# Attention, an expert network and a cosine network in one kernel: the merged unit goes last, and conversions, weights' jobs and pair products stand in other places

## The chip, the cores and the metric

The kernel runs on one core of a Trainium2 chip. The time is the device time of one execution in microseconds (us). A kernel's time is the median of several executions; one further execution is recorded by the profiler, and every row below comes from that one.

## What is computed

Three stages follow each other; the output of each is the input of the next (all float32 for the reader; `w_in` and `w_out` come as float64).

```python
scores = scale * np.matmul(q, k.transpose(0, 1, 3, 2))      # B=2, H=8, S=576, D=64
scores = np.where(mask, scores + bias[None], -1000000000.0) # causal window of 128, ALiBi slopes
attn = softmax(scores); x = attn @ v                        # -> 1152 tokens x 512
for e in range(4):                                          # w1[e] 512x1024, w2[e] 1024x512
    h = np.maximum(x @ w1[e], 0.0)
    out += p[:, e:e + 1] * (h @ w2[e])                      # p: normalised domain_probs
h = out @ w_in                                              # 512 x 2048
result = (h * np.cos(h)) @ w_out                            # 2048 x 512
```

## The kernel before

**Precision.** Every operand of the two networks is held as two parts, a high part that TensorE takes and a low part, the remainder. A product is three passes (high-high, high-low, low-high), so that 128 contraction rows of a 128x512 result cost three matmuls. The high part is a ScalarE copy, the low part a subtract (`sub`, L162), on DVE for some and on GpSimd for others.

**Tokens.** The 1152 tokens are nine units of 128 (`UNITS`, `place`): unit 0 holds the first 64 rows of both batches, merged; units 1 to 4 are the rest of batch 0, units 5 to 8 the rest of batch 1. The networks use the same nine as tiles; tiles 1 to 4 and 5 to 8 are the two halves of a 2x2 block product.

**Attention.** Each unit has two steps (`steps`, four heads each). In a software pipeline, step k computes its scores (`att_scores`, L418), the transposes of the probabilities come two steps later, the product with the values another one later, and the unit's normalised result (L530) is then transposed and cut into the operands of the networks (`own`, `transform`). Between these pieces `fill(k, s)` puts other work by a table of steps: the jobs that cut the weights (k 4 to 19), the transposed constants, and the first products of group 0.

**The two networks.** The first one runs in groups 0 to 7 (four experts, halves of F1), the second in groups 8 to 11 (quarters of 2048); each group has 512 hidden columns. A group has these parts:
- Two `pair`s (j = 0, 1), layer one for tiles 1 to 8 in Winograd's form: seven products A11, A12, S1, S2, S3, S4, A22 of six matmuls 128x512 each (L647, `product`). A11 and A12 add into the same PSUM bank; between them ScalarE copies the bank into p1 (L717). DVE forms u1, c22 and the final sums (L711). `finish` makes the hidden values: a ReLU in the first network; in the second a cosine chain of six stages (`cosine`, L595: two ScalarE steps, DVE's L604, ScalarE's sine L608, DVE's product with h, then ScalarE's high part L620 and GpSimd's low part L162).
- `left`: layer one of tile 0, two blocks of twelve matmuls 128x256 (L677), and `turn_rows` ("X" in the tables): its four transposes (L703) and the cut into parts.
- `layer2` per tile, twelve matmuls (L787), then one DVE sum into `acc` (L808, L814). In the second network `ahead` ("a5" to "a8") does half of tiles 5 to 8 early.

The operands named in the rows: `xs` and `xz` are the cut token operands, `w1t` and `w2t` the cut weights, `hpair` and `h0` the hidden values of tiles 1 to 8 and of tile 0, `x0` the operands of tile 0.

**What sets the order.** `tc.manual_schedule()` keeps the order of the code on each engine. `steps(g)` yields a list of (step, stages, njobs, ncv), and `run` (L974) issues for each: the first half of the step (its matmuls), `stages` stages of every open cosine chain, `njobs` weights' jobs, `ncv` steps of conversions, then the second half (its copies and sums). A weights' job is a ScalarE part and a GpSimd subtract, with a raw load on the SyncE queue. A conversion (`convert`, L254) turns the 64-bit words of `w_in` and `w_out` into float32 in DRAM: a load on the SyncE queue into one of two buffers, ScalarE L272 and L284, DVE L274, L278, L282 and L287 in four steps, and a store; 32 of them have to be done by the end of group 6, since the second network's weights are read from there.

**The turn.** In group 7 the accumulated tiles are the input of the second network: `flip` ("f0" to "f7", then `last_flip`) transposes a finished tile and cuts it like the attention's units, between the layer-two steps of that group.

## Time and profile before

| | |
|---|---|
| three runs | 686.02, 686.30, 689.27 us; median 686.3 |
| the profiled execution | 689.04 us; its span 687.3 us |
| TensorE (PE) busy | 651.2 us, 95% of the span; weight loads (PEld) 77% |
| VectorE (DVE) busy | 453.6 us, 66% |
| ScalarE (ACT) busy | 329.6 us, 48% |
| GpSimd (POOL) busy | 350.8 us, 51% |
| mean granted TensorE clock | 0.987 of 2.4 GHz |

A row of a timeline reads: start, duration, engine, line, operation, output<-input, shape, how many instructions stand in the row; in brackets the idle time of the engine before it, the engine that ended that wait, and what it wrote. The modelled end of a matmul row can lie some 0.15 us behind the start of the next row, since matmuls are pipelined; so the time between two starts is what a row costs.

### The profile page before, as it was taken

Reading aid. Unit: us, or ns where it says so; the run is one execution under the profiler, and the core shown is the slowest. Engines: PE = TensorE matmul, PEld = TensorE weight load, DVE = VectorE, ACT = ScalarE, POOL = GpSimd, SP = SyncE. Lnnn points to the kernel's source line nnn. Section 1 sums busy time; section 2 is a strip of 40 time slices with the busy share of each in tenths; the row PEclk is TensorE's granted clock in tenths of the full one; section 3 lists DMA queues with packets and bytes.
Section 4 is the critical chain, followed back from the end, with each engine's and each line's share of the span. In section 5 each row is a group of like instructions: output and inputs, shape, how many; then the busy total and the mean of one; then the engine's idle time right before and its main releaser. Section 6 shows DMA issues by size and latency. Waiting matters only on the chain.

```text
span 687.3 us, 9161 instructions
## 1 busy us (share of the span) xinstructions
PE 651.2 (95%) x3332; PEld 528.9 (77%) x3332; DVE 453.6 (66%) x778; ACT 329.6 (48%) x687; POOL 350.8 (51%) x330
## 2 busy tenths in 40 slices
PE   8999979999899999999999999998999989989988
PEld 6776758888688888788788888886777677767766
DVE  5778968968868878868773624557844743753652
ACT  5877534553353453444442422556663654653640
POOL 2755617365255274174364561753487377368340
PEclk9999999999999999999999999999999999999999
DMA  7441204625615516446231210110102102001003
GB/s 240 115 138 48 65 28 137 215 62 181 187 31 185 183 51 224 124 124 196 78 123 47 61 62 31 37 56 0 31 1 92 31 0 93 31 1 61 17 5 118
DMA packets 38957, 60.38 MB, mean 88 GB/s; under 512 B 4608, under 2 KB 21248, under 8 KB 38912
## 3 DMA queue, kind: packets, MB, share of 16 engines
q1 hardware_dynamic: 38912, 59.80, 27.2%
q8 instruction: 26, 0.43, 0.3%
q14 instruction: 19, 0.16, 0.1%
HBM read 49.04 MB, written 10.75 MB: 87 GB/s over the span
## 4 chain that ended last, share of the span: by engine, by line
PE 42%; DVE 22%; ACT 12%; DMA 8%; issue 7%; POOL 7%; SPq 1%; POOLq 0%; DVEq 0%; ACTq 0%
PE o_ps L787 20%; PE o_ps L647 15%; DMA cr<-w_in 5%; DMA cr<-w_out 4%; POOL w1t L162 2%; PE o_ps L677 2%; DVE o_ps L711 2%; DVE cv L278 2%; DVE c L711 2%; DVE cv L282 2%; DVE hpair L637 2%; ACT p L435 2%; POOL w2t L162 2%; ACT hpair L636 2%; ACT u L608 1%
## 5 line engine op out<-in xcount | busy, mean ns | idle before, releaser
L787 PE MATMUL o_ps<-w2t,hpair 128*128 128x512 f32 x1140 | 270.7, 393 | 6.0 <-POOL hpair L162 5.0
L787 PEld LDWEIGHTS o_ps<-w2t,hpair 128*128 128x128 f32 x1140 | 212.3, 189 | 50.8 <-POOL hpair L162 6.8
L647 PE MATMUL o_ps<-xs,w1t 128*128 128x512 f32 x720 | 173.8, 397 | 10.5 <-ACT p L717 7.3
L647 PEld LDWEIGHTS o_ps<-xs,w1t 128*128 128x128 f32 x720 | 136.4, 191 | 42.5 <-ACT p L717 10.2
L162 POOL TENSOR_TENSOR w1t<-raw,w1t 128x512 fp32r<-128x512 f32 x48 | 63.7, 1342 | 102.1 <-ACT w1t L185 101.8
L162 POOL TENSOR_TENSOR w2t<-raw,w2t 128x512 fp32r<-128x512 f32 x48 | 66.7, 1406 | 81.9 <-ACT w2t L185 81.6
L647 PE MATMUL o_ps<-xz,w1t 128*128 128x512 f32 x288 | 72.5, 401 | 8.1 <-DVE c L711 7.7
L162 POOL TENSOR_TENSOR w1t<-sm,w1t 128x512 fp32r<-128x512 f32 x48 | 64.1, 1345 | 20.6 <-ACT w1t L185 19.0
L647 PEld LDWEIGHTS o_ps<-xz,w1t 128*128 128x128 f32 x288 | 54.3, 192 | 24.4 <-DVE c L711 12.3
L162 POOL TENSOR_TENSOR hpair<-u,hpair 128x512 fp32r<-128x512 f32 x32 | 42.8, 1355 | 54.6 <-ACT hpair L620 54.6
L808 DVE SCALAR_TENSOR_TENSOR accpair<-o_ps,pr,accpair 128x512 f32<-128x512 f32 x56 | 41.6, 744 | 32.9 <-PE o_ps L787 32.9
L637 DVE SCALAR_TENSOR_TENSOR hpair<-o_ps,hpair 128x512 fp32r<-128x512 f32 x48 | 32.9, 688 | 21.6 <-ACT hpair L636 21.5
L185 ACT ACTIVATE w1t<-sm 128x512 fp32r<-128x512 f32 x44 | 27.4, 626 | 39.5 <-POOL sm L162 39.5
L272 ACT ACTIVATE cr<-cr 128x512 int32<-128x512 uint32 x32 | 21.7, 679 | 48.9 <-DMA cr<-w_out 24.8
L636 ACT ACTIVATE hpair<-o_ps 128x512 fp32r<-128x512 f32 x48 | 28.5, 597 | 33.6 <-DVE o_ps L711 33.0
L604 DVE SCALAR_TENSOR_TENSOR u<-r,u 128x512 f32<-128x512 f32 x36 | 33.8, 938 | 15.2 <-ACT r L601 15.1
L677 PE MATMUL o_ps<-w1t,x 128*128 128x256 f32 x288 | 39.9, 285 | 1.9 <-POOL w1t L162 1.9
L435 ACT ACTIVATE p<-p,nmax 128x256 f32<-128x256 f32 (+2 forms) x72 | 33.5, 468 | 16.5 <-DVE nmax L429 16.5
L677 PEld LDWEIGHTS o_ps<-w1t,x 128*128 128x128 f32 x288 | 37.7, 191 | 4.5 <-POOL w1t L162 2.9
L284 ACT ACTIVATE cr<-cr 128x512 f32<-128x512 f32 x32 | 21.7, 678 | 37.8 <-DVE cv L278 37.7
L814 DVE TENSOR_TENSOR accpair<-o_ps,accpair 128x512 f32<-128x512 f32 x23 | 15.9, 690 | 36.1 <-PE o_ps L787 36.1
L711 DVE TENSOR_TENSOR o_ps<-o_ps,u 128x512 f32<-128x512 f32 x48 | 33.2, 691 | 6.7 <-PE o_ps L647 6.7
(134 smaller groups left out, 895.7 us busy)
## 6 DMA issues: line engine op xcount, KB each, us to landing
raw<-w SPq DMA_DIRECT2D x32, 512.0 KB, 3.7
cr<-w_in SPq DMA_DIRECT2D x16, 512.0 KB, 4.4
cr<-w_out SPq DMA_DIRECT2D x16, 512.0 KB, 4.4
wi<-cv SPq DMA_DIRECT2D x16, 256.0 KB, 3.4
wo<-cv SPq DMA_DIRECT2D x16, 256.0 KB, 2.2
raw<-wi SPq DMA_DIRECT2D x8, 512.0 KB, 3.4
raw<-wo SPq DMA_DIRECT2D x8, 512.0 KB, 3.6
qt<-qT SPq DMA_DIRECT2D x9, 256.0 KB, 2.9
```

The source lines that it names most:

```text
L162: eng.tensor_tensor(out=out, in0=a, in1=b, op=ALU.subtract)
L185: nc.scalar.activation(out=out, in_=src, func=AF.Copy)
L272: nc.scalar.activation(out=lw, in_=lw.bitcast(U32), func=AF.Copy, scale=2.0 ** -29)
L435: nc.scalar.activation(out=p[:, k, :wid], in_=p[:, k, :wid], func=AF.Exp, scale=-1.0, bias=nmax[:, k : k + 1], accum_out=den[:, k, 0:1],)
L604: nc.vector.scalar_tensor_tensor(out=u, in0=r, scalar=MAGIC, in1=u, op0=ALU.subtract, op1=ALU.subtract)
L636: nc.scalar.activation(out=hi, in_=src, func=AF.Relu)
L637: nc.vector.scalar_tensor_tensor(out=lo, in0=src, scalar=0.0, in1=hi.bitcast(F32), op0=ALU.max, op1=ALU.subtract)
L647: nc.tensor.matmul(ps, w(a, k, m), operand_of_x(bb, b)[:, m], start=(start and m == 0 and (a, bb) == PASSES[0]), stop=(stop and m == 1 and ...
L677: nc.tensor.matmul(ps[:, j * 256 : (j + 1) * 256], x0[:, bb, d, :], w_t[1, g, j][:, a, 0, d * 256 : (d + 1) * 256], start=(d == 0 and (a, ...
L711: add = lambda out, a, b: nc.vector.tensor_tensor(out=out, in0=a, in1=b, op=ALU.add)
L787: nc.tensor.matmul(ps, hidden(a, f, t), w_t[2, g, f // 2][:, bb, f % 2, :], start=(f == 0 and (a, bb) == PASSES[0]), stop=(f == NFG - 1 an ...
L808: nc.vector.scalar_tensor_tensor(out=o, in0=ps, scalar=s, in1=o, op0=ALU.mult, op1=ALU.add)
```

## The change

1. The attention's units run in the order 1 to 8, then 0. Unit 1 is loaded in halves, its keys on the ScalarE queue; unit 0's keys have a tile of their own (`kh`). The small bias `bm0` is built at k = 9, the identity before that.
2. Group 0's left rows, their transposes, the routing and tile 0's layer two leave the attention and stand in `steps(0)`; the pairs of group 0 start at k = 18 and 19.
3. `pair` has three kinds: 0 puts A12 after S3 (groups 1 to 7, as before), 1 puts it right after A11 (groups 0 and 8), 2 after S2 and u1 (groups 9 to 11, which had it right after A11).
4. In groups 9 and 10 two weights' jobs stand in the second pair in place of beside "a5" and "a6".
5. At the turn, the left rows of group 8 leave the tiles and stand in `last_flip`, between the first products of both pairs; their transposes ("X") and tile 0's layer two stand inside group 8's pairs.
6. Conversions stand only beside the tiles and left rows that the table `ncv` names, none beside tiles 3 and 4 and "X": 23 steps in a group.

```diff
+        make_identity(nc, ident)
+
+    def first_bias():
+
         for b in range(2):
             r = slice(64 * b, 64 * b + 64)
             nc.gpsimd.tensor_copy(bm0[r], bm[r, :, WIN + 64 * b : WIN + 64 * b + 64])
-        make_identity(nc, ident)
...
     def load_unit(u):
...
         if u == 0:
+            nc.sync.dma_start(out=qt, in_=blocks(qT, 0, 128))
+            kh = qvp.tile([128, B, ND, 64], F32, name="kh", tag="qt")
...
+                nc.sync.dma_start(out=kh[:, b], in_=head(b))
+            heads.append(kh)
+            return
...
+        for h in (slice(0, 2), slice(2, 4)) if u == 1 else (slice(0, ND),):
+            nc.sync.dma_start(out=qt[:, h], in_=blocks(qT, u, 128)[:, h])
+            queue = nc.scalar if u == 1 else nc.sync
+            queue.dma_start(out=kt[:, h, s0 : s0 + n], in_=blocks(kT, u, 128)[:, h])
+            if i == 1:
+                queue.dma_start(out=kt[:, h, :64], in_=head(b)[:, h])
...
     def own(t, x1):
 
         hi, lo = parts(t)
+        if t < NP and mm is None:
+            yield
+            yield
         hi(B11, x1[:, 0:2])
         yield
...
-    units = range(1 + 2 * NP)
+    units = [*range(1, 1 + 2 * NP), 0]
...
-    def pair(g, j, early=False):
+    def pair(g, j, early=0):
 
         w = operand(w_t[1, g, j])
         c = lambda name: cp.tile([128, NB], F32, name=name, tag="c")
@@ -716,7 +734,7 @@
         p1 = p1p.tile([128, NB], F32, name="p1", tag="p1")
         nc.scalar.activation(out=p1, in_=pa, func=AF.Copy)
         yield
-        if early:
+        if early == 1:
             product(pa, w, A12, B21, False, True)
             yield
             finish(g, pa, f, 1)
@@ -727,6 +745,11 @@
         u1 = c("u1")
         add(u1, pb, p1)
         yield
+        if early == 2:
+            product(pa, w, A12, B21, False, True)
+            yield
+            finish(g, pa, f, 1)
+            yield
         pc = sums()
         product(pc, w, S1, T1, True, True)
         yield
@@ -872,7 +895,6 @@
             )
         load_units_to(2)
         constants()
-        first = left(0)
         early = {}
 
         def fill(k, s):
@@ -884,23 +906,17 @@
             if (k, s) == (2, 0):
                 for _ in range(RAWS):
                     loads_ahead()
-            if (k, s) == (4, 0):
+            if (k, s) == (6, 0):
                 nc.sync.dma_start(out=pr, in_=probs.rearrange("(t p) e -> p t e", p=128))
-            if (k, s) == (11, 0):
-                routing()
+            if (k, s) == (9, 0):
+                first_bias()
             if s == 0 and 4 <= k < 20:
                 next(jobs)
-            if (k, s) in ((8, 1), (10, 1)):
-                next(first)
             step = None
-            if (k, s) == (10, 2):
-                whole(first)
-            if (k, s) == (13, 1):
-                step = turn_rows(0)
-            if s == 1 and k in (18, 19):
-                step = early[k - 18] = pair(0, k - 18, True)
-            if (k, s) == (20, 2):
-                step = layer2(0, 0, ps_s.tile([128, DM], F32, name="s_ps", tag="s_ps"))
+            if (k, s) == (18, 1):
+                step = early[0] = pair(0, 0, 1)
+            if (k, s) == (19, 1):
+                next(early[0])
             if step:
                 next(step)
             move(24 if (k, s) == (20, 2) else (0, 3, 2)[s])
@@ -923,53 +939,73 @@
 
         last, turn = g == NG1 + NG2 - 1, g == NG1 - 1
         moe = g < NG1
+        early_kind = 1 if g in (0, NG1) else 0 if moe else 2
+        ps = [early.pop(j, None) or pair(g, j, early_kind) for j in range(2)]
         if g == 0:
-            seq = [0, 1] + [0] * 5 + [1] * 5
-            more = [0] * 7 + [1] * 5
+            next(ps[0])
+            yield ps[1], 1, 0, 0
+            yield ps[1], 1, 0, 0
+            first = left(0)
+            yield half(first, False), 1, 0, 0
+            yield half(first, True), 1, 0, 0
+            seq = [0, 0, "X", 0, 0, 0, 1, 1, 1, 1, 1]
+            more = [0] * 6 + [1] * 5
+            routing()
         elif g == NG1:
-            seq = [1, 0, 1] + [0] * 5 + [1] * 5
-            more = [0] * 4 + [1, 1, 0, 0] + [0] * 5
+            seq = [0, 0, 0, 0, "X", 0, 1, 1, "0", 1, 1, 1]
+            more = [0, 1, 1, 0, 0, 0, 1, 1, 0, 0, 0, 0]
+        elif moe:
+            seq = [0] * 7 + [1] * 7
+            more = [0, 1, 1, 0, 0, 0, 0] + [0, 1, 1, 1, 1, 1, 1]
         else:
-            seq = [0] * 7 + [1] * 7
-            more = [0, 1, 1, 0, 0, 0, 0] + [0] + [moe] * 6
-        ps = [early.pop(j, None) or pair(g, j, g == 0 or not moe) for j in range(2)]
-        for k, (j, m) in enumerate(zip(seq, more)):
-            if not moe and k == len(seq) - seq[::-1].index(0):
-                yield layer2(g, 0), 2, 0, 0
-            yield ps[j], 1, int(m), 0
+            seq = [0] * 7 + ["0"] + [1] * 7
+            more = [0, 1, 1, 0, 0, 0, 0, 0] + ([0] * 7 if last else [0, 1, 1, 0, 0, 0, 0])
+        for j, m in zip(seq, more):
+            if j == "X":
+                yield turn_rows(g), 2, m, 0
+            elif j == "0":
+                yield layer2(g, 0), 2, m, 0
+            else:
+                yield ps[j], 1, m, 0
         nxt = None if last else left(g + 1)
+        ncv = {0: 2, "La": 3, 5: 3, 6: 3, 1: 3, 7: 3, "Lb": 2, 2: 2, 8: 2}
         if turn:
-            order = (0, 1, "f0", 5, "f1", 2, "f5", "La", 6, "f2", "Lb", 3, "f6", 4, "f3", 7, "X", "f4", 8, "f7")
+            order = (0, 1, "f0", 5, "f1", 2, "f5", 6, "f2", 3, "f6", 4, "f3", 7, "f4", 8, "f7")
             njobs = [2, 2, 0, 2, 0, 2]
         elif moe:
-            order = (() if g == 0 else (0,)) + ("La", 5, 6, 1, 7, "Lb", 2, 8, 3, "X", 4)
+            order = (0, "La", 5, 6, 1, 7, "Lb", 2, 8, 3, "X", 4)
             njobs = [2] + [1] * 7 if g == 0 else [1] * 8
         elif last:
             order, njobs = ("a5", "a6", "a7", "a8", 5, 6, 7, 8, 1, 2, 3, 4), []
         else:
             order = ("a5", "a6", "a7", "a8", "La", 5, 6, 7, "Lb", 8, 1, 2, "X", 3, 4)
-            njobs = [1, 1, 0, 0, 1, 1, 1, 1, 1, 1, 1, 1, 1, 1, 2]
+            njobs = [0, 0, 0, 0, 1, 1, 1, 1, 1, 1, 1, 1, 1, 1, 2]
         for k, o in enumerate(order):
             m = njobs.pop(0) if njobs else 0
             if isinstance(o, int):
                 assert o == 0 or not any(c > 0 for c, _ in chains)
-                yield layer2(g, o), 2, m, 3 if o == 5 else 2
+                yield layer2(g, o), 2, m, ncv.get(o, 0)
             elif o[0] == "f":
                 yield flip(int(o[1])), 0, m, 0
             elif o[0] == "a":
                 yield ahead(g, int(o[1])), 2 if last else 1, m, 0
             elif o[0] == "L":
-                yield half(nxt, o == "Lb"), 2, m, 2
+                yield half(nxt, o == "Lb"), 2, m, ncv.get(o, 0)
             else:
-                yield turn_rows(g + 1), 2, m, 1
+                yield turn_rows(g + 1), 2, m, 0
         if turn:
-            yield from last_flip(g + 1)
-
-    def last_flip(g):
-
-        early[0] = pair(g, 0, True)
+            yield from last_flip(g + 1, nxt)
+
+    def last_flip(g, nxt):
+
+        early.update({j: pair(g, j, 1) for j in range(2)})
         yield early[0], 0, 0, 0
         yield flip(2 * NP), 0, 0, 0
+        yield early[1], 0, 0, 0
+        yield half(nxt, False), 0, 0, 0
+        yield early[0], 1, 0, 0
+        yield half(nxt, True), 0, 0, 0
+        yield early[1], 2, 0, 0
 
     def run(groups):
         for g in groups:
```

**How the order moves.** Numbers behind a name tell buffers apart.

TensorE, first pair of group 10, before (`o_ps` are PSUM banks, w1t the group's first cut weights):

```order
L647 MATMUL o_ps_5162<-xs_132,w1t_4966 128x512 x12
L647 MATMUL o_ps_5184<-xs_132,w1t_4966 128x512 x6
L647 MATMUL o_ps_5197<-xs_132,w1t_4966 128x512 x6
L647 MATMUL o_ps_5207<-xs_132,w1t_4966 128x512 x6
L647 MATMUL o_ps_5197<-xz_1003,w1t_4966 128x512 x6
L647 MATMUL o_ps_5207<-xz_1003,w1t_4966 128x512 x6
L787 MATMUL o_ps_5244<-w2t_5154,h0_140 128x512 x6
```

TensorE, the same place, after:

```order
L665 MATMUL o_ps_5168<-xs_132,w1t_4897 128x512 x6
L665 MATMUL o_ps_5177<-xs_132,w1t_4897 128x512 x6
L665 MATMUL o_ps_5168<-xs_132,w1t_4897 128x512 x6
L665 MATMUL o_ps_5203<-xs_132,w1t_4897 128x512 x6
L665 MATMUL o_ps_5212<-xs_132,w1t_4897 128x512 x6
L665 MATMUL o_ps_5203<-xz_872,w1t_4897 128x512 x6
L665 MATMUL o_ps_5212<-xz_872,w1t_4897 128x512 x6
```

Before, A11 and A12 stand in one row of twelve on one bank, then S2, S1, S3, S4, A22. After, S2 (o_ps_5177) stands between A11 and A12 (both o_ps_5168), and the other four keep their order.

DVE, from the last tiles of group 2 to the first pair of group 3, before (`cr` and `cv` are conversion buffers, L808 the sums of tiles, L162 the low part of tile 0's hidden values, L711 the pair's sums):

```order
L282 ISA cv_2374<-cr_2331,cv_2374 128x1024
L808 SCALAR_TENSOR_TENSOR accpair_1284<-o_ps_2379,pr_138,accpair_1284 128x512
L287 SCALAR_TENSOR_TENSOR cv_2374<-cr_2331,cv_2374 128x512
L162 TENSOR_TENSOR h0_140<-l_ps_2395,h0_140 128x512
L274 TENSOR_SCALAR cv_2419<-cr_2372 128x512
L278 SCALAR_TENSOR_TENSOR cv_2419<-cr_2372,cv_2419 128x512
L282 ISA cv_2419<-cr_2372,cv_2419 128x1024
L808 SCALAR_TENSOR_TENSOR accpair_1284<-o_ps_2403,pr_138,accpair_1284 128x512
L711 TENSOR_TENSOR u1_2444<-o_ps_2434,p1_2432 128x512
L711 TENSOR_TENSOR c22_2457<-o_ps_2446,u1_2444 128x512
```

DVE, the same place, after:

```order
L302 SCALAR_TENSOR_TENSOR cv_2349<-cr_2320,cv_2349 128x512
L289 TENSOR_SCALAR cv_2390<-cr_2347 128x512
L293 SCALAR_TENSOR_TENSOR cv_2390<-cr_2347,cv_2390 128x512
L831 SCALAR_TENSOR_TENSOR accpair_1235<-o_ps_2373,pr_138,accpair_1235 128x512
L831 SCALAR_TENSOR_TENSOR accpair_1235<-o_ps_2395,pr_138,accpair_1235 128x512
L177 TENSOR_TENSOR h0_140<-l_ps_2409,h0_140 128x512
L831 SCALAR_TENSOR_TENSOR accpair_1235<-o_ps_2416,pr_138,accpair_1235 128x512
L729 TENSOR_TENSOR u1_2449<-o_ps_2439,p1_2437 128x512
L729 TENSOR_TENSOR c22_2462<-o_ps_2451,u1_2449 128x512
L729 TENSOR_TENSOR c22_2462<-o_ps_2464,c22_2462 128x512
```

Before, four conversion instructions stand after the sum on o_ps_2379 and ahead of u1; after, the last one stands ahead of four sums, and between it and u1 stand only those and the parts of tile 0's hidden values.

TensorE, the end of the attention, before (L520 is the values' product of unit 8, s_ps_1231 tile 0's layer two, the rows of L647 are A11 and A12 of both pairs, S2, S1 and S3):

```order
L520 MATMUL x_ps_1205<-pt_1177,vt_893 64x128 x2
L520 MATMUL x_ps_1205<-pt_1177,vt_1005 64x128 x2
L787 MATMUL s_ps_1231<-w2t_1028,h0_140 128x512 x6
L787 MATMUL s_ps_1231<-w2t_1125,h0_140 128x512 x6
L647 MATMUL o_ps_1142<-xs_132,w1t_353 128x512 x2
L647 MATMUL o_ps_1190<-xs_132,w1t_460 128x512 x6
L647 MATMUL o_ps_1306<-xs_132,w1t_353 128x512 x6
L647 MATMUL o_ps_1315<-xs_132,w1t_353 128x512 x6
L647 MATMUL o_ps_1324<-xs_132,w1t_353 128x512 x6
```

TensorE, the same place, after (L527 is the merged unit's values' product, L695 group 0's left rows, L721 their transposes):

```order
L527 MATMUL x_ps_1183<-pt_1118,v0_190 64x64 x4
L527 MATMUL x_ps_1183<-pt_1123,v0_190 64x64 x4
L527 MATMUL x_ps_1183<-pt_1155,v0_190 64x64 x4
L527 MATMUL x_ps_1183<-pt_1160,v0_190 64x64 x4
L665 MATMUL o_ps_1243<-xs_132,w1t_465 128x512 x12
L695 MATMUL o_ps_1260<-w1t_360,x0_133 128x256 x12
L695 MATMUL o_ps_1260<-w1t_465,x0_133 128x256 x12
L665 MATMUL o_ps_1291<-xs_132,w1t_360 128x512 x6
L665 MATMUL o_ps_1300<-xs_132,w1t_360 128x512 x6
L721 MATMUL l_ps_1309<-ident_126,lt_1285 128x128 x4
L665 MATMUL o_ps_1316<-xs_132,w1t_360 128x512 x6
```

Before, tile 0's layer two stands between the last unit and the rest of the first products. After, the merged unit's values' product is the attention's last, group 0's left rows stand between the first products of the second pair and S2, and their transposes between S1 and S3.

## Rows read from the trace of the kernel before

**Rows 1.** TensorE's timeline in group 10; columns as told above.

```profile
579.28 1.52 PE L647 MATMUL o_ps<-xs,w1t 128*128 128x512 f32 x6
581.49 5.73 PE L647 MATMUL o_ps<-xs,w1t 128*128 128x512 f32 x24 [0.69 <-ACT p L717]
587.53 3.04 PE L647 MATMUL o_ps<-xz,w1t 128*128 128x512 f32 x12 [0.31 <-DVE c L711]
590.41 2.88 PE L787 MATMUL o_ps<-w2t,h 128*128 128x512 f32 x12
593.13 1.52 PE L647 MATMUL o_ps<-xs,w1t 128*128 128x512 f32 x6
595.63 5.74 PE L647 MATMUL o_ps<-xs,w1t 128*128 128x512 f32 x24 [0.98 <-ACT p L717]
...
604.55 5.60 PE L787 MATMUL o_ps<-w2t,hpair 128*128 128x512 f32 x24
...
610.93 0.98 PE L677 MATMUL o_ps<-w1t,x 128*128 128x256 f32 x6 [0.54 <-POOL w1t L162]
...
614.66 3.92 PE L787 MATMUL o_ps<-w2t,hpair 128*128 128x512 f32 x16 [1.26 <-POOL hpair L162]
...
632.61 1.52 PE L647 MATMUL o_ps<-xs,w1t 128*128 128x512 f32 x6
```

**Rows 2.** All engines' timeline in group 10: rows of DVE and GpSimd.

```profile
599.19 2.98 POOL L162 TENSOR_TENSOR hpair<-u,hpair 128x512 fp32r<-128x512 f32 x2 [1.64 <-ACT hpair L620]
599.37 1.66 DVE L604 SCALAR_TENSOR_TENSOR u<-r,u 128x512 f32<-128x512 f32 x1
...
600.95 0.68 DVE L711 TENSOR_TENSOR c<-o_ps,u 128x512 f32<-128x512 f32 x1
...
604.58 0.68 DVE L604 SCALAR_TENSOR_TENSOR u<-r,u 128x512 f32<-128x512 f32 x1
...
609.14 3.00 POOL L162 TENSOR_TENSOR w1t<-raw,w1t 128x512 fp32r<-128x512 f32 x2
...
612.09 3.76 POOL L162 TENSOR_TENSOR hpair<-u,hpair 128x512 fp32r<-128x512 f32 x3
```

**Rows 3.** TensorE's timeline, the start of two neighbouring groups of the first network.

```profile
373.57 6.96 PE L647 MATMUL o_ps<-xs,w1t 128*128 128x512 f32 x30
...
420.50 6.96 PE L647 MATMUL o_ps<-xs,w1t 128*128 128x512 f32 x30
```

**Rows 4.** TensorE's timeline at the turn, start of group 8.

```profile
478.60 7.32 PE L647 MATMUL o_ps<-xs,w1t 128*128 128x512 f32 x24 [2.27 <-ACT p L717]
```

**Rows 5.** TensorE's waits, 130 to 440 us (total, times, longest); one from its timeline.

```profile
PE o_ps L647 <- DVE c L711: 4.9, 3, 2.6
...
188.01 4.60 PE L647 MATMUL o_ps<-xz,w1t 128*128 128x512 f32 x12 [2.57 <-DVE c L711]
```

**Rows 6.** DVE's timeline ahead of that hole; DVE's waits from 150 to 186 us.

```profile
185.82 0.74 DVE L808 SCALAR_TENSOR_TENSOR accpair<-o_ps,pr,accpair 128x512 f32<-128x512 f32 x1
...
DVE cv L274 <- DMA cr<-w_out: 2.4, 1, 2.4
```

**Rows 7.** Windows: length, busy PE PEld DVE ACT POOL, granted clock, DMA share, GB/s.

```profile
184.00:192.00 8.00, 5.43 (x18) 3.99 (x17) 6.31 (x9) 1.71 (x3) 1.35 (x1) 0.79 0.41 116
478.00:486.00 8.00, 7.32 (x24) 5.56 (x24) 5.74 (x8) 5.19 (x12) 2.69 (x3) 0.79 0.00 0
```

**Rows 8.** DVE's timeline in the attention: the normalisations of units 5 and 8.

```profile
58.43 0.68 DVE L530 TENSOR_TENSOR x<-x_ps,rs 128x512 f32<-128x512 f32 x1
...
83.75 0.68 DVE L530 TENSOR_TENSOR x<-x_ps,rs 128x512 f32<-128x512 f32 x1
```

**Rows 9.** TensorE's timeline from the start to group 1's left rows.

```profile
9.62 1.65 PE L418 MATMUL s_ps<-k,qt 64*128 64x192 f32 x8
...
89.54 5.95 PE L647 MATMUL o_ps<-xs,w1t 128*128 128x512 f32 x18 [3.17 <-ACT hpair L636]
...
105.88 1.59 PE L677 MATMUL o_ps<-w1t,x 128*128 128x256 f32 x12
```

More of the change, by code (lines that the diff above doesn't have):

```diff
@@ L120, in place, with blocks, head @@
         return (u - 1) // NP, (u - 1) % NP + 1
+    def blocks(a, u, n):
+        return a[:, u * ND * 128 : u * ND * 128 + ND * n].rearrange("p (m n) -> p m n", m=ND)
+    def head(b):
+        o = b * ND * 64
+        return kT[:, o : o + ND * 64].rearrange("p (m n) -> p m n", m=ND)
+    heads = []
     def load_unit(u):
-        q_t[u] = qvp.tile([128, ND, 128], F32, name="qt", tag="qt")
-        cols = slice(u * ND * 128, (u + 1) * ND * 128)
-        nc.sync.dma_start(out=q_t[u], in_=qT[:, cols].rearrange("p (m n) -> p m n", m=ND))
+        qt = q_t[u] = qvp.tile([128, ND, 128], F32, name="qt", tag="qt")
@@ L413, in att_scores @@
                             ps[hh][c, m, :wid], q_t[u][r, 2 * g + m, c],
-                            k_t[b][r, 2 * g + m, :64], start=True, stop=True,
+                            heads[0][r, b, 2 * g + m], start=True, stop=True,
                         )
@@ L447, in att_sums @@
         nc.vector.tensor_reduce(
-            out=rec, in_=dens[:, u % 2], axis=mybir.AxisListType.X, op=ALU.add
+            out=rec, in_=dens[:, units.index(u) % 2], axis=mybir.AxisListType.X, op=ALU.add
         )
```

32 lines of the change are left out of this document (13 added, 19 removed).

## The prediction

> **What bounds the kernel now.** I read the stretches first, then TensorE's timeline for every place where a row starts later than the row before it ends, then the engine that the waiting row names, on its own timeline.
>
> In a middle group of the first network TensorE has no hole: from one group's first product to the next's is 420.50 − 373.57 = 46.93 us [rows 3], and twelve 128x512 products take 593.13 − 590.41 = 2.72 us, 0.227 each [rows 1]. That is all its work, so 46.93 is the floor of a group. A group of the second network takes 632.61 − 579.28 = 53.33 [rows 1]: 6.4 us of holes, in a group that has the same products. Three kinds make them up.
> - After A11 (six products, 1.36 us) A12 should start at 580.64 and starts at 581.49: 0.85. It adds into the bank that ScalarE is still copying (p1). In the second pair it is 595.63 − 594.49 = 1.14.
> - S4 waits for DVE's c22: 24 products from 581.49 end at 586.93, S4 starts at 587.53: 0.60, in both pairs; each hole costs some 0.15 more at the restart. DVE was late because the cosine's L604 stood ahead of c22 and took 1.66 us beside a GpSimd subtract, against about 0.7 otherwise [rows 2].
> - The next left rows wait for w1t (0.69 and 0.55 around 610.93), and tile 5's second half waits for the hidden low part until 614.66 (1.45). GpSimd did two w1t subtracts at 609.14, ahead of the low parts at 612.09 [rows 1, 2].
>
> In the first network three of the seven later groups have a hole, 4.9 us in all [rows 5], each from DVE reaching c22 late: it reads tile 4's sum only at 185.82, after conversion steps that themselves waited 2.4 us for a load [rows 6], and TensorE goes on at 188.01, after which twelve products take 4.60 instead of about 3.0. The granted clock is 0.79 of 2.4 GHz there (part of the stretch at 1.2), after a hole of 2.6 us [rows 5, 7]. With the clock and the restarts I count 7.4 us lost there. The turn to the second network has the same pattern: a hole of 2.27 at 478.60 and 24 products in 7.32 (floor 5.44) at 0.79 [rows 4, 7].
>
> In the attention TensorE runs without holes in its first half, and DVE sets the pace in the second: its normalisation of unit 5 starts at 58.43, that of unit 8 at 83.75 [rows 8], and S2 of group 0 waits until 89.54 [rows 9].
>
> **The change part by part.**
>
> *Kind 2 pairs (groups 9 to 11).* S2 now stands between A11 and A12, so p1 (0.6 us) is hidden by 1.36 us of products: −0.85 and −1.14. c22 stands ahead of L604 on DVE, and S3 still lies between S1 and S4: c22 takes 0.7 of those 1.36, so the 0.60 goes in the first pair. Four restarts of 0.15 go too: 0.6.
>
> *Two weights' jobs from behind the pairs into the second pair (groups 9, 10).* w1t is then ready before the left rows: −0.69 − 0.55. The price: GpSimd's two subtracts (1.25 to 1.5 each [rows 2]; 1.3 taken) lie beside the second pair, and L604 takes 1.66 there rather than 0.68, one microsecond in front of the second add of c22, on which A22 waits. Of that S4 hides about 0.35, so about 0.65 of the second 0.60 is given back. Tile 5's low part now has two w1t subtracts less ahead of it (2.6 us on GpSimd, about 1.0 of copies on ScalarE), but TensorE comes 4.5 us sooner: in the trace of before the low part is there 614.66 − 604.40 = 10.3 us after A22's end, without those jobs about 8, plus the 1.0 from L604; TensorE needs it 5.44 + 1.43 + 0.45 = 7.3 after A22. I keep a wait of 1.7, a little over the 1.45 of now. Sum for one group: 0.85 + 1.14 + 0.60 + 0.6 + 1.24 + (0.60 − 0.65) − 0.25 = 4.1, with the smaller restart costs 4.3. Bounds: 5.5 (DVE's add is not delayed, low part at 7.8) and 2.5 (the low part comes no sooner against the clock on the wall). Two groups: **−8.6**, from −11 to −5.
>
> *Group 11* has no jobs for later groups: the same without w1t, 0.85 + 1.14 + 1.2 + 0.6, and tile 5's wait changes little: **−4**, from −5.8 to −2.
>
> *Turn and group 8.* The left rows (two blocks of 1.43) and the transposes of their result leave the turn's tiles and stand between A11, A12 and their twins. From the last flip to S2 TensorE then has A11', left, A12, left, A12': 1.36 × 3 + 1.43 × 2 = 6.9 us of work, where it now stands still for 2.27 (and loses 7.32 − 5.44 = 1.9 to the clock and restart) [rows 4, 7]. That hole goes, 4.2. Against it: the cosine of the left rows now stands on DVE and ScalarE in front of c22 (two more L604 of 0.7, two more ScalarE steps each of 0.6), so S4 of the first pair waits about 1.7; and the turn's flips follow each other faster by 3.3 us, over which DVE, busy some 5.5 of each 6.1 us, may lose 1. The wait for tile 5's low part (1.3 there too) and the one behind S4 shrink by 1 each, and so does the 0.3 at the left rows' transposes. I take **−4.5**, from −7 to −2.
>
> *Conversions with early tiles only (groups 0 to 4).* 23 steps instead of 24 a group, none beside tiles 3 and 4 and the transposes between. The steps are the same instructions, and DVE is in order; the sum of its work falls by one step (0.7 to 1.4 us). What moves is the order: after the last step DVE now has the reads of tiles 8, 3 and 4 and then u1 and c22, and no load of a conversion can hold these up. Today three to five conversion instructions, one of them behind a load of 2.4, stand there. I expect c22 to come 1 to 2.5 us sooner against TensorE. Of the three holes two are near 1.2 and go; the third of 2.6 shrinks to about 1 and then costs no clock. **−5**, from 0 (the loads, two buffers deep, set the end of the steps wherever they stand) to −7.4.
>
> *The merged unit last.* Before unit 1's scores at 9.62 lie the merged unit's scores [rows 9]; with its transposes and its values' products it takes TensorE about 6 us, and the left rows of group 0 inside the attention 2 × 1.43 (a row of twelve takes 1.59 with the end of the last [rows 9]) and their transposes 0.4. All this no longer stands ahead of unit 5: its normalisation, 58.43 now, comes at about 48.5 [rows 8]. From there DVE sets the pace: 83.75 − 58.43 = 25.3 to unit 8, plus the merged unit's own steps on DVE (two rounds of eight short passes and copies, about 2), plus 5 for unit 8's transform: the merged unit is normalised at about 81. Then x0's two parts (ScalarE 0.6, GpSimd 1.3), A12' waiting behind them on ScalarE, and left rows of 2.86 stand in front of S2: 87 to 88, against 89.54. A hole of 3 to 4 us before A12' stays, as now, with the clock at its lower level after it. But tile 0's layer two (2.72) and the transposes (0.44), which are done by then now, come after S2. So the left rows of group 1 at 105.88 move to about 104.4: **−1.5**. Bounds: −5 if the second half is less DVE-bound than the 25.3 say, +3 if the start gains only the merged unit's own 6. The keys of unit 1 on ScalarE's queue, the halves of its loads and the identity built before the small bias lie in front of the first score, and I count them in the 10.
>
> The sum: −1.5 − 5 − 4.5 − 8.6 − 4 = −23.6. The profiled execution took 689.0 (span 687.3), so 665.4; two of the three other runs were at 686.0 and 686.3, so this execution may hold 2.7 that the median does not, and part of that may be among the holes counted here. I take 665.
>
> **A rule against this change.** L604 with two inputs in SBUF took 1.66 beside a GpSimd subtract; DVE's adds with one input in PSUM stayed near 0.7 [rows 2]. The Trainium skill, "SBUF — State Buffer", section "Who interferes with whom", says that a VectorE instruction with two SBUF inputs contends with a GpSimd instruction that reads SBUF, and that whichever starts first holds the port for its whole length while the other is blocked. By that rule the moved jobs can also be the ones that wait. The row agrees on the slowdown of DVE; which one is blocked in the second pair no row of before can show.
>
> **The rivals.**
> 1. *The low parts become the bound.* Jobs and low parts queue on GpSimd in the second pair, each of the two w1t subtracts and of the four L604 holds up the other by 1.0 to 1.3, and tile 5 waits for what the pair saved: groups 8 to 11 keep 1 to 2 us each, not 4. For it: GpSimd would be busy without a break there; against: its eight low parts and two jobs are 13 us in 24. Time: 665.4 + 4 × 2.5 = 675. Chance 0.17. (The rule above would act in this way.)
> 2. *The conversions do not come earlier.* Their loads set the pace, the three holes stay: 665.4 + 5 = 670. Chance 0.12. A stronger form of it is the slower side: packed three to a tile, each of the six conversions of a group, not one or two, waits 2.4 for its load [rows 6]. That is 4 × 2.4 = 9.6 us more on DVE per group in five groups; with 18.6 saved elsewhere the kernel is slower than now as soon as DVE loses 3.7 a group, and at 9.6 the time is 665.4 + 5 + 48 = 718. Against it: the tiles without steps give DVE 6 us to catch up. Chance 0.04.
> 3. *More from the attention.* The second half is TensorE's again, S2 starts near 82 at the full clock: 665.4 − 5 − 2 = 658. Chance 0.12.
>
> **How the numbers follow.** My forecast (660 to 669) has 0.49, rivals 1, 2 and 3 together 0.41, the slow form 0.04, something that I did not see 0.06 (0.04 of it near no change, 0.01 on either side). From 657 to 677 holds rival 3 and rival 1 and leaves the slow forms out. Faster by over 0.5% (about what the measurement can tell from no change), that is under 682.9: 0.91; within: 0.04; slower: 0.05.
>
> **What would show it.** In the profile after: a second-network group of about 49 us (53.33 now), no wait of the product after A11 on p1, and a wait of under 2.5 us on the hidden low part; first-network groups 1 to 5 at 46.9 to 48; no hole at the first S2 of group 8, but one of 1 to 2 at its S4; the first left rows of group 1 near 104. I am wrong if c22 is late again in the first network, if the low parts' wait grows beyond 3 us, or if S2 of group 0 starts after 90.

## The result and the profile after

The changed kernel takes 669.56 us (median; 668.5 to 672.75) against 686.75 before: a ratio of 0.975, interval 0.971 to 0.979. 665 was forecast, in a range from 657 to 677. The profiled execution took 668.5 us (span 666.7), 20.5 less than the profiled one of before; that pair lies 3 us wider apart than the medians.

Cut at the same marks (group 1's first product, group 7's, group 9's, group 11's), the two traces and one more of the unaltered changed kernel (experiment 6) say where the time went:

| stretch | before | after | after, again | forecast change | seen |
|---|---|---|---|---|---|
| start to group 1 | 131.55 | 136.29 | 135.45 | −1.5 | +4.7, +3.9 |
| groups 1 to 6 | 288.95 | 283.91 | 287.01 | −5 | −5.0, −1.9 |
| group 7 (the turn) and 8 | 105.44 | 100.44 | 100.42 | −4.5 | −5.0, −5.0 |
| groups 9 and 10 | 106.67 | 96.16 | 96.22 | −8.6 | −10.5, −10.5 |
| group 11 to the end | 54.7 | 49.9 | 51.5 | −4 | −4.8, −3.2 |

The median lies 4.6 us above the 665. The attention lost 4 to 5 us where a gain of 1.5 was forecast, the second network gained some 2 more than forecast, and groups 1 to 6 gained between 2 and 5. That the time fell inside the range, just above the 660 to 669 held likeliest, is in part luck: errors of opposite sign met.

**Group 10 of the second network**, TensorE's timeline of the changed kernel (columns as for [rows 1], which these rows answer):

```profile
568.71 6.96 PE L665 MATMUL o_ps<-xs,w1t 128*128 128x512 f32 x30
575.51 2.88 PE L665 MATMUL o_ps<-xz,w1t 128*128 128x512 f32 x12
...
580.95 6.96 PE L665 MATMUL o_ps<-xs,w1t 128*128 128x512 f32 x30
587.75 3.18 PE L665 MATMUL o_ps<-xz,w1t 128*128 128x512 f32 x12
590.77 5.60 PE L810 MATMUL o_ps<-w2t,hpair 128*128 128x512 f32 x24
596.21 1.59 PE L695 MATMUL o_ps<-w1t,x 128*128 128x256 f32 x12
...
598.86 3.91 PE L810 MATMUL o_ps<-w2t,hpair 128*128 128x512 f32 x16 [0.59 <-POOL hpair L177]
...
616.80 6.96 PE L665 MATMUL o_ps<-xs,w1t 128*128 128x512 f32 x30
```

The waits on p1 and w1t are gone, and so is the one on c22 but for some 0.3 in the second pair (587.75); each pair's first 30 products stand in one row of 6.96, as in the first network [rows 3]. One wait of 0.59 is left on tile 5's low part, where [rows 1] had 1.26. The group takes 616.80 − 568.71 = 48.09 us.

**The turn**, the same view (to be read against [rows 4]):

```profile
469.26 1.64 PE L665 MATMUL o_ps<-xs,w1t 128*128 128x512 f32 x6
470.74 1.59 PE L695 MATMUL o_ps<-w1t,x 128*128 128x256 f32 x12
472.16 1.55 PE L665 MATMUL o_ps<-xs,w1t 128*128 128x512 f32 x6
473.55 1.59 PE L695 MATMUL o_ps<-w1t,x 128*128 128x256 f32 x12
474.98 5.63 PE L665 MATMUL o_ps<-xs,w1t 128*128 128x512 f32 x24
...
493.36 1.66 PE L665 MATMUL o_ps<-xz,w1t 128*128 128x512 f32 x6 [0.56 <-DVE c L729]
```

The left rows fill the hole of 2.27, the 24 products behind it take 5.63 and not 7.32, and the only wait that the timeline still shows in group 8's pairs is 0.56, at the second pair's last product (A22).

**The end of the attention**, the same view (against [rows 9]), and the windows view of ten microseconds of it (columns as for [rows 7]):

```profile
77.68 1.15 PE L527 MATMUL x_ps<-pt,v 64*64 64x64 f32 x32
82.79 2.93 PE L665 MATMUL o_ps<-xs,w1t 128*128 128x512 f32 x6 [3.96 <-DVE x L548]
86.41 2.93 PE L665 MATMUL o_ps<-xs,w1t 128*128 128x512 f32 x6 [0.69 <-ACT p L735]
89.13 3.73 PE L695 MATMUL o_ps<-w1t,x 128*128 128x256 f32 x24
92.70 2.91 PE L665 MATMUL o_ps<-xs,w1t 128*128 128x512 f32 x12
...
110.52 1.60 PE L695 MATMUL o_ps<-w1t,x 128*128 128x256 f32 x12
```

```profile
82.00:92.00 10.00, 8.52 (x31) 6.83 (x32) 2.81 (x8) 2.31 (x4) 1.27 (x1) 0.56 0.26 86
```

VectorE's timeline has the row that ends the hole:

```profile
82.06 0.68 DVE L548 TENSOR_TENSOR x<-x_ps,rs 128x512 f32<-128x512 f32 x1
```

The hole of 3.96 stands ahead of A11' (the second pair's A11), which waits for this normalisation of the merged unit. Behind it the granted clock is 0.56 of 2.4 GHz, a mean of its two levels (1.2 and 2.4): six products take 2.93 instead of 1.36. S2 starts at 92.70 (89.54 before), group 1's left rows at 110.52 (105.88).

**The first network** has lost its waits on c22 and has a new one. ScalarE's and TensorE's rows from the timeline of all engines, group 2's end:

```profile
227.88 0.67 ACT L287 ACTIVATE cr<-cr 128x512 int32<-128x512 uint32 x1 [2.00 <-DMA cr<-w_in]
...
228.44 0.58 ACT L704 ACTIVATE lt<-o_ps 128x512 f32<-128x512 f32 x1
...
229.08 0.66 PE L721 MATMUL l_ps<-ident,lt 128*128 128x128 f32 x4 [1.86 <-ACT lt L704]
```

The transposes of the left rows wait for ScalarE's copy `lt`, and that copy stands on ScalarE behind a conversion that has just waited 2.00 for its load. The other five stretches between the first products of groups 1 to 7 are 46.9 to 47.1 in this trace.

### The profile page after: what moved, and what is told of

Its sections match the earlier page's. It is cut to its first block, busy times and chain, and to the rows that moved or that the text cites. A ratio compares the mean times of both kernels' runs of the same rounds, so it can differ in the third digit from the quotient of the medians.

```text
span 666.7 us, 9161 instructions
## 1 busy us (share of the span) xinstructions
PE 644.9 (97%) x3332; PEld 527.3 (79%) x3332; DVE 449.0 (67%) x778; ACT 327.9 (49%) x687; POOL 348.3 (52%) x330
## 4 chain that ended last, share of the span: by engine, by line
PE 71%; ACT 10%; DVE 10%; DMA 4%; issue 3%; POOL 1%; ACTq 0%; POOLq 0%; SPq 0%; DVEq 0%
PE o_ps L810 34%; PE o_ps L665 28%; PE o_ps L695 3%; DMA cr<-w_out 2%; ACT p L453 1%; PE s_ps L436 1%; ACT u L618 1%; ACT r L619 1%; DVE c L729 1%; DMA cr<-w_in 1%; ACT u L626 1%; ACT hpair L638 1%; PE x_ps L538 1%; PE t_ps L501 1%; DVE hpair L655 1%
## 5 line engine op out<-in xcount | busy, mean ns | idle before, releaser
L665 PE MATMUL o_ps<-xs,w1t 128*128 128x512 f32 x720 | 172.0, 394 | 4.7 <-DVE x L548 4.0
L177 POOL TENSOR_TENSOR w2t<-raw,w2t 128x512 fp32r<-128x512 f32 x48 | 64.4, 1361 | 63.2 <-ACT w2t L200 62.8
L665 PE MATMUL o_ps<-xz,w1t 128*128 128x512 f32 x288 | 70.9, 392 | 1.6 <-DVE c L729 1.5
L622 DVE SCALAR_TENSOR_TENSOR u<-r,u 128x512 f32<-128x512 f32 x36 | 30.7, 853 | 14.3 <-ACT r L619 14.3
L695 PEld LDWEIGHTS o_ps<-w1t,x 128*128 128x128 f32 x288 | 38.4, 195 | 1.9
L695 PE MATMUL o_ps<-w1t,x 128*128 128x256 f32 x288 | 38.8, 286 | 0.0
L302 DVE SCALAR_TENSOR_TENSOR cv<-cr,cv 128x512 f32<-128x512 f32 x32 | 36.9, 1154 | 1.8 <-ACT cr L299 0.7
```

The source lines that it names most:

```text
L177: eng.tensor_tensor(out=out, in0=a, in1=b, op=ALU.subtract)
L302: nc.vector.scalar_tensor_tensor(out=fl(o), in0=fl(hw), scalar=TINY, in1=fl(a), op0=ALU.is_ge, op1=ALU.mult,)
L622: nc.vector.scalar_tensor_tensor(out=u, in0=r, scalar=MAGIC, in1=u, op0=ALU.subtract, op1=ALU.subtract)
L665: nc.tensor.matmul(ps, w(a, k, m), operand_of_x(bb, b)[:, m], start=(start and m == 0 and (a, bb) == PASSES[0]), stop=(stop and m == 1 and ...
L695: nc.tensor.matmul(ps[:, j * 256 : (j + 1) * 256], x0[:, bb, d, :], w_t[1, g, j][:, a, 0, d * 256 : (d + 1) * 256], start=(d == 0 and (a, ...
```

## The experiments

"Marks" are starts on TensorE's timeline of the run's own profile. Ratios are to the kernel before on the same chip.

**1. The pairs' order: A12 right after A11 again in groups 9 to 11.**

```diff
-        early_kind = 1 if g in (0, NG1) else 0 if moe else 2
+        early_kind = 0 if 0 < g < NG1 else 1
```

> The changed kernel with A12 right after A11 again in groups 9 to 11 (kind 1), the two jobs staying in the second pair. Theory: the waits on p1 come back (0.85 and 1.14 a group with the restart), and c22 is late by 0.6 to 1 in both pairs again, so a group takes 48.1 + 3 = 51 us and the time is about 669.6 + 9 = 678. Rival: what the pairs lose, the wait on tile 5's low part (0.59 now) gives back, and the group takes 49.5 to 50: 675.

679.89 us, ratio 0.987 (0.984 to 0.991). TensorE's timeline of group 10:

```profile
574.33 5.73 PE L665 MATMUL o_ps<-xs,w1t 128*128 128x512 f32 x24 [0.69 <-ACT p L735]
580.37 3.03 PE L665 MATMUL o_ps<-xz,w1t 128*128 128x512 f32 x12 [0.31 <-DVE c L729]
...
588.47 5.74 PE L665 MATMUL o_ps<-xs,w1t 128*128 128x512 f32 x24 [0.99 <-ACT p L735]
594.53 3.02 PE L665 MATMUL o_ps<-xz,w1t 128*128 128x512 f32 x12 [0.32 <-DVE c L729]
...
605.91 3.96 PE L810 MATMUL o_ps<-w2t,hpair 128*128 128x512 f32 x16 [1.02 <-POOL hpair L177]
```

All four waits of [rows 1] on p1 and c22 are back. From A11 at 572.12 to the next at 623.88 a group takes 51.76, 3.7 more than 48.09, and so does group 9; group 11 takes 3.4 more (53.3). Theory borne out: by the marks the order alone is worth 10.8 us. By the ratios (0.987 against 0.975; the unaltered changed kernel did not run on this chip) it is some 8. The wait on tile 5's low part grew (1.02 for 0.59), so the rival's giving back did not happen.

**2. The two jobs: beside "a5" and "a6" again in groups 9 and 10.**

```diff
-            more = [0, 1, 1, 0, 0, 0, 0, 0] + ([0] * 7 if last else [0, 1, 1, 0, 0, 0, 0])
+            more = [0, 1, 1, 0, 0, 0, 0, 0] + [0] * 7
...
-            njobs = [0, 0, 0, 0, 1, 1, 1, 1, 1, 1, 1, 1, 1, 1, 2]
+            njobs = [0 if g == NG1 else 1, 0 if g == NG1 else 1, 0, 0, 1, 1, 1, 1, 1, 1, 1, 1, 1, 1, 2]
```

> The changed kernel with the two weights' jobs of groups 9 and 10 beside a5 and a6 again, pairs of kind 2. Theory: the left rows wait for w1t again (0.69 and 0.55 a group, or more, since TensorE now comes 4.5 us sooner), and tile 5's low part, behind two more subtracts of 1.3, makes a wait of 2.5 to 3.5 out of 0.59; a group takes 48.1 + 1.2 + 2.5 = 51.8 and the time is about 677. Rival: the slower cosine passes of VectorE in the second pair (1.42 and 0.98 instead of 0.68) cost what the move gains; the groups take 48 to 49 and the time is 670 to 671.

675.43 us, ratio 0.980 (0.976 to 0.984). TensorE's timeline:

```profile
549.35 0.74 PE L695 MATMUL o_ps<-w1t,x 128*128 128x256 f32 x4 [1.17 <-POOL w1t L177]
...
551.82 3.92 PE L810 MATMUL o_ps<-w2t,hpair 128*128 128x512 f32 x16 [1.27 <-POOL hpair L177]
...
569.77 6.96 PE L665 MATMUL o_ps<-xs,w1t 128*128 128x512 f32 x30
...
599.87 0.75 PE L695 MATMUL o_ps<-w1t,x 128*128 128x256 f32 x4 [1.16 <-POOL w1t L177]
...
602.34 6.73 PE L810 MATMUL o_ps<-w2t,hpair 128*128 128x512 f32 x16 [1.27 <-POOL hpair L177]
```

The wait on w1t is back (1.17), the one on the low part 1.27, not the 2.5 to 3.5 that I expected. Group 9 takes 569.77 − 519.25 = 50.5, not 51.8. Group 10 takes 53.3, since the clock falls behind the same two holes there (sixteen products in 6.73, not 3.92; granted clock 0.60 from 602 to 610) and not in group 9. The move is worth 2.4 us a group at full clock. It does not add up with the order: 3.7 + 2.4 is 6.1, and a group of the changed kernel is 5.24 shorter than before. The slower cosine that I had priced against it is in the changed kernel's timeline (all engines, group 10's second pair):

```profile
586.78 1.29 POOL L177 TENSOR_TENSOR hpair<-u,hpair 128x512 fp32r<-128x512 f32 x1
...
587.20 1.42 DVE L622 SCALAR_TENSOR_TENSOR u<-r,u 128x512 f32<-128x512 f32 x1
...
588.03 1.74 POOL L177 TENSOR_TENSOR w1t<-raw,w1t 128x512 fp32r<-128x512 f32 x1
```

L622 (L604 before) starts during the subtract of 586.78 and takes 1.42 rather than 0.68; the subtract of 588.03 starts during L622 and takes 1.74 rather than 1.29. The later one was lengthened each time. TensorE loses 0.3 to it, in its wait for c22: the row at 587.75 takes 3.18, the one at 575.51 2.88. The Trainium skill, "SBUF — State Buffer", section "Who interferes with whom", says that the order of issue decides which of the two is blocked; these rows agree.

**3. The attention: as before, the rest changed.** The edit puts back the units' order, the loads, `own`, `fill` and group 0's list.

```diff
-    units = [*range(1, 1 + 2 * NP), 0]
+    units = range(1 + 2 * NP)
...
-            yield half(first, False), 1, 0, 0
-            yield half(first, True), 1, 0, 0
-            seq = [0, 0, "X", 0, 0, 0, 1, 1, 1, 1, 1]
+            seq = [0, 1] + [0] * 5 + [1] * 5
```

> The changed kernel with the attention, its loads and group 0's order put back as before (merged unit first, left rows and tile 0's layer two inside the attention); pairs, jobs, turn and conversions stay changed. Theory from the two traces' marks: group 1's left rows start at 110.52 in the changed kernel and at 105.88 before, so this part alone cost 4.6 us, and with it undone the mark returns to about 105.9 and the time falls from 669.6 to about 665. Rival (the prediction's): the merged unit at the end gains 1.5, the later mark has another cause, and undoing it gives about 671.

670.95 us, ratio 0.974 (0.970 to 0.978): no difference from the changed kernel, as the rival said. But the mark of group 1's left rows moved as the theory said, to 105.66. What ate it, on the timeline of all engines:

```profile
121.25 0.67 ACT L272 ACTIVATE cr<-cr 128x512 int32<-128x512 uint32 x1 [3.66 <-DMA cr<-w_in]
...
121.83 0.62 ACT L185 ACTIVATE w1t<-raw 128x512 fp32r<-128x512 f32 x1
...
122.50 0.80 PE L677 MATMUL o_ps<-w1t,x 128*128 128x256 f32 x2 [3.63 <-ACT w1t L185]
```

With TensorE earlier by 4.9, the second left rows of group 1 come before their weights, whose first part stands on ScalarE behind a conversion that waits 3.66 for its load. The granted clock is 0.50 from 122 to 128, and group 1's first product comes at 137.90, 1.6 later than in the changed kernel. So the time alone could not tell the attention's cost; a kernel without such waits was needed (experiment 8).

**4. A11' inside the attention.** Its operands are tiles 1 to 4, long there; only its bank was in question, since the banks of `mm` replace those of the attention.

```diff
+            if (k, s) == (20, 1):
+                step = early[1] = pair(0, 1, 1)
...
             next(ps[0])
             yield ps[1], 1, 0, 0
-            yield ps[1], 1, 0, 0
```

> The changed kernel, but the second pair's first product A11' of group 0 is issued inside the attention, ahead of the merged unit's last values' product, in the PSUM bank that the first pair leaves free. Theory: A11' at 82.79 waited 4.0 us not for its operands but for a bank that the merged unit's normalisation frees; A11' and A12' then run before and in that hole, at the full clock, S2 of group 0 starts near 88.4 (92.70 now), group 1's left rows near 106 (110.52 now), the time is about 665.5. Rival: VectorE's finish of unit 8 and the merged unit bounds the place, the hole moves whole to the left rows, the clock is low for them and the two first sums, S2 starts at 91 or later, the time is 668 to 670.

666.14 us, ratio 0.967 (0.964 to 0.971). TensorE's timeline:

```profile
78.64 1.65 PE L665 MATMUL o_ps<-xs,w1t 128*128 128x512 f32 x6
80.22 0.68 PE L527 MATMUL x_ps<-pt,v 64*64 64x64 f32 x16
82.32 2.55 PE L665 MATMUL o_ps<-xs,w1t 128*128 128x512 f32 x6 [1.41 <-ACT p L735]
84.66 3.98 PE L695 MATMUL o_ps<-w1t,x 128*128 128x256 f32 x24
88.48 2.91 PE L665 MATMUL o_ps<-xs,w1t 128*128 128x512 f32 x12
...
106.31 1.60 PE L695 MATMUL o_ps<-w1t,x 128*128 128x256 f32 x12
```

A11' runs at 78.64, ahead of the normalisation for which it had waited: its operands were there, the bank was not. S2 starts at 88.48, the left rows at 106.31, within 0.1 and 0.3 of the expectation; in this trace the clock falls behind the shorter hole too (2.55 for six products, 3.98 for the left rows' 24).

**5. The conversions: the old table.**

```diff
-                yield layer2(g, o), 2, m, ncv.get(o, 0)
+                yield layer2(g, o), 2, m, 0 if o == 0 and g == 0 else 3 if o == 5 else 2
...
-                yield half(nxt, o == "Lb"), 2, m, ncv.get(o, 0)
+                yield half(nxt, o == "Lb"), 2, m, 2
...
-                yield turn_rows(g + 1), 2, m, 0
+                yield turn_rows(g + 1), 2, m, 1
```

> The changed kernel with the conversions spread as before: two steps beside each tile and each half of the left rows, three beside tile 5, one beside the transposes. Theory (the prediction's): conversion steps stand in front of u1 and c22 again, c22 comes late in two or three of groups 1 to 6 by 1 to 2.6 us, and the time goes from 669.6 to about 674.5; the wait of the transposes on the left rows' copy (1.9 at 229.08) goes. Rival: the loads of the conversions set the pace wherever the steps stand, only the place of the holes changes, and the time stays within 1 us of 669.6.

**6. The changed kernel itself, on the same chip.**

> The changed kernel itself, unaltered, for comparison on the same chip: 668 to 672.

672.51 us, ratio 0.977 (0.974 to 0.981), for the old table; 672.34, ratio 0.976 (0.973 to 0.979), for the changed kernel. The times agree with the rival; intervals this wide would hide a difference of 3 us. TensorE's waits from 130 to 425 us (total, times, longest), first with the old table, then the changed kernel:

```profile
PE o_ps L665 <- DVE c L729: 3.5, 2, 3.2
PE o_ps L665 <- ACT p L735: 0.8, 1, 0.8
```

```profile
PE l_ps L721 <- ACT lt L704: 3.5, 3, 2.7
```

The waits moved from c22 on VectorE to `lt` on ScalarE. Groups 1 to 6 take 287.1 and 287.0 us. The other five traces with the new table (the first one of the changed kernel, experiments 1 to 4) have 283.9, 284.0, 284.2, 283.9 and 286.6; the old table has this one trace. Its longest wait:

```profile
194.25 3.01 PE L665 MATMUL o_ps<-xz,w1t 128*128 128x512 f32 x12 [3.23 <-DVE c L729]
```

The granted clock behind it stayed at 1.00 (194 to 200). In the second trace of the changed kernel the longest wait on `lt` was 2.67, and the clock fell behind it:

```profile
229.24 0.66 PE L721 MATMUL l_ps<-ident,lt 128*128 128x128 f32 x4 [2.67 <-ACT lt L704]
229.65 4.58 PE L810 MATMUL o_ps<-w2t,hpair 128*128 128x512 f32 x12
```

In the first trace the wait was 1.86 and twelve products behind it took 2.99. These waits hang on when loads land, so they differ between executions.

**7. The conversions spread over seven groups**, on top of experiment 4.

```diff
-        ncv = {0: 2, "La": 3, 5: 3, 6: 3, 1: 3, 7: 3, "Lb": 2, 2: 2, 8: 2}
+        ncv = {0: 2, "La": 2, 5: 3, 6: 2, 1: 3, 7: 3, "Lb": 0, 2: 2, 8: 2}
```

> The kernel with A11' of group 0 inside the attention, and besides that 19 conversion steps a group over seven groups in place of 23 over less than six, none beside the second half of the left rows. Theory: ScalarE reached the left rows' copy 10 us after TensorE, because conversions that wait for their loads stood ahead of it on its queue; with less of them the waits of the transposes (3.1 us in the kernel with A11' alone) fall below 0.5 and the time goes from 666 to about 663. Rival: the loads are late because they stand behind the raw loads on the SyncE queue, and the waits stay: 666.

661.79 us, ratio 0.962 (0.959 to 0.964). Groups 1 to 6 take 281.5 us without a wait on TensorE; one of them in the windows view, and TensorE's row at group 0's A12' (where experiment 4 had 2.55):

```profile
178.50:225.40 46.90, 46.90 (x221) 39.30 (x220) 35.28 (x49) 19.61 (x34) 23.97 (x20) 1.00 0.40 125
```

```profile
82.87 1.65 PE L665 MATMUL o_ps<-xs,w1t 128*128 128x512 f32 x6 [1.40 <-ACT p L735]
```

ScalarE's conversions still wait for loads there (1.45 and 1.81 in group 2), but `lt` no longer comes late. Four conversion steps fewer in a group, and none beside the second left rows: both were changed at once, and which of them does it was not told apart.

**8. The attention's price without those waits:** the changed kernel with experiment 7's table alone, and with it the attention as before (experiment 3's edit).

> The changed kernel with the conversions spread over seven groups (19 steps a group) and nothing else: A11' of group 0 waits for its bank again. With the first network at its floor (281.5 us for groups 1 to 6) the parts can be told apart without the scatter of its holes. Theory: the early A11' is worth 4.2 us by the marks, so this kernel takes 661.8 + 4 = 666. Rival: the spread alone brought the gain, and the time is 663 or less.

> The kernel with the attention and group 0 as before, everything else changed, and the conversions spread over seven groups (19 steps a group, 17 in group 0). Theory: the merged unit at the end costs 4.6 us at group 1's first left rows, and what gave it back in the run without the spread was a wait of 3.6 on the cut weights behind conversions; without that wait the time is 661 to 662, some 4.5 below the changed kernel with the spread alone. Rival: the wait on the cut weights comes again, since conversions stand in the same places in group 0, and the time is 665 to 667, as for the new attention.

665.70 us, ratio 0.970 (0.966 to 0.973), with the new attention, and 661.17, ratio 0.964 (0.960 to 0.968), with the old one, on the same chip, both as expected. TensorE's timelines, new, then old:

```profile
84.04 2.93 PE L665 MATMUL o_ps<-xs,w1t 128*128 128x512 f32 x6 [3.97 <-DVE x L548]
...
112.10 1.59 PE L695 MATMUL o_ps<-w1t,x 128*128 128x256 f32 x12
```

```profile
89.58 5.92 PE L647 MATMUL o_ps<-xs,w1t 128*128 128x512 f32 x18 [3.14 <-ACT hpair L636]
...
105.85 1.59 PE L677 MATMUL o_ps<-w1t,x 128*128 128x256 f32 x12
```

Both groups 1 to 6 are at 281.5, so the difference is the attention's: the merged unit at the end costs 4.5 us by the medians, 5.7 by the marks of group 1's first product (137.25 against 131.59).

**9. The turn and group 8 as before:** first in the changed kernel, then on top of experiment 7. With the order of the turn go back group 8's list, its two jobs and `last_flip`.

```diff
-            order = (0, 1, "f0", 5, "f1", 2, "f5", 6, "f2", 3, "f6", 4, "f3", 7, "f4", 8, "f7")
+            order = (0, 1, "f0", 5, "f1", 2, "f5", "La", 6, "f2", "Lb", 3, "f6", 4, "f3", 7, "X", "f4", 8, "f7")
```

> The changed kernel with the turn and group 8 put back as before (left rows and their transposes among the turn's tiles, only the first pair's product A11 before the last flip, jobs of group 8 in their old places). Theory: the hole of 2.3 us at group 8's S2 comes back with the low clock behind it, the stretch from group 7's first product to group 9's is 105.4 us as before (100.4 in the changed kernel), the time about 674.6. Rival: the hole was made by what preceded it in the old kernel and the low part of tile 5 gives some back: 103, 672.

> The kernel with A11' inside the attention and the conversions spread, and the turn and group 8 put back as before. Theory: the stretch from group 7's first product to group 9's is 105.4 us as in the kernel before (100.5 with the change), so 661.8 + 5 = 666.8. Rival: the low part of tile 5 and the waits on c22 shrink in its place, 103 us, 664.5.

674.72 us, ratio 0.981 (0.978 to 0.983), beside 672.34 for the changed kernel on that chip: 2.4 us, half of the 5 expected, between kernels whose groups 1 to 6 scatter by 3 from trace to trace. On top of experiment 7 it is 665.22, ratio 0.969 (0.965 to 0.973), where experiment 7 had 0.962. In the second one's trace the stretch from group 7 to group 9 is 517.74 − 412.22 = 105.5 us against 100.5 in experiment 7's; TensorE's row at group 8's S2:

```profile
470.37 7.32 PE L665 MATMUL o_ps<-xs,w1t 128*128 128x512 f32 x24 [2.27 <-ACT p L735]
```

It is the row of [rows 4] to the hundredth. Theory borne out there: 5.0 us, for the whole part. The hole and the clock behind it are 4.2, the wait on tile 5's low part in group 8 another 1.2 (none in the changed kernel's trace); against them stands the 0.56 at A22.

**10. The left rows of group 0 behind S2 and S1**, on top of experiment 7.

```diff
-            yield half(first, False), 1, 0, 0
-            yield half(first, True), 1, 0, 0
-            seq = [0, 0, "X", 0, 0, 0, 1, 1, 1, 1, 1]
+            seq = [0, 0, "A", "B", 0, "X", 0, 0, 1, 1, 1, 1, 1]
```

> The kernel with A11' inside the attention and the conversions spread, and the left rows of group 0 behind S2 and S1 instead of ahead of them, so that TensorE has work while GpSimd cuts the merged unit's operand. Theory: the wait of 1.0 on that operand goes, group 1's first left rows start at 105.4 (106.4), the time is 660.8. Rival: S2 waits for the bank that the merged unit's normalisation frees, or S3 for VectorE, and nothing is gained: 661.8.

661.05 us, ratio 0.962 (0.958 to 0.966): no measurable difference from experiment 7. In the trace the wait of 0.96 on the merged unit's low part is gone, and group 1's left rows start at 104.47 (106.42 in experiment 7; 0.75 of the difference stands ahead of the edit already). It is, with experiment 7 and the old attention with experiment 7's table, the fastest seen, 8 us below the changed kernel.

## Why the forecast held, and where it did not

- **The pairs of kind 2** [rows 1, 2]: right in mechanism and nearly in size. 0.85 + 1.14 + 0.60 + 0.6 was said for the order itself (3.2), and 3.7 came, 0.4 of it from the longer wait on the low part.
- **The jobs** (rival 1, and the wait of 1.7 at tile 5): mis-sized. The second pair's wait of 0.6 was thought to come back through the slower L604 (0.65); it did slow to 1.42, but S4 hid all but 0.3. The low part's wait was taken as 1.7 and was 0.59. So a group gave 5.24, not 4.3. The step that failed reckoned the low part 1.0 later for L604's sake: it came 598.86 − 590.62 = 8.2 us after A22's end, the "about 8" of the forecast without that 1.0.
- **Turn and group 8** [rows 4]: −5.0 for −4.5. The predicted wait of 1.7 at the first pair's S4 did not come; what came was 0.56 at the second pair's A22; no run shows why.
- **The conversions** [rows 5, 6]: the step said that no load can hold up u1 and c22 any more, and that was so; that the time of the holes comes back did not follow. The loads' lateness is carried by whatever stands behind a conversion on either engine, and ScalarE's queue was not followed: `lt` and w1t stand there. The old and the new table give the same time within 3 us (experiments 5 and 6). Rival 2, at 0.12, was nearest: the loads stay late, though the holes did not stay on c22 but moved to `lt`. That the time came close to its 670 is no proof of it, since the attention's loss alone would bring it there. The −5.0 of the profiled pair is the favourable end: the traces with the new table lie between −5.0 and −1.9.
- **The merged unit last** [rows 8, 9]: wrong in sign, and the step of the forecast that failed in mechanism. The normalisations came as forecast: unit 5 at 48.45 (48.5 forecast) and the merged unit at 82.06 (81). The hole of 4 was forecast as well, but ahead of A12'. It stood ahead of A11', because the attention's banks are only free after the last unit, and A11' is the first product in the new banks. So A11', A12' and the left rows (1.36 + 1.36 + 2.86 = 5.6 us at the full clock) all ran behind the hole, with 0.69 for p1 between, from 82.79 to 92.70, most of it at the low clock: S2 came 5 us after the 87 to 88 of the forecast. In the second trace of the changed kernel only A11' ran at the low clock (2.92, then 1.66 for A12'), and S2 came at 91.88. The term's upper bound of +3 was too low for both (+4.7, +3.9). The forecast named "S2 of group 0 after 90" as a sign of being wrong, and it was one. With A11' inside the attention and the left rows behind S2 and S1 (experiment 10) the mark is at 104.47, the "about 104.4" of the forecast.

What stays open: why a load of the conversions lands late (the raw loads stand on the same SyncE queue, and no run took them away), and whether fewer conversion steps or their absence beside the second left rows cured `lt`.
